# The third unit's q turned behind the second unit's first scores, where three idle products stood

## The chip, the cores and the metric

The kernel runs on one core of one Trainium2 chip. The metric is device time in microseconds (us) of one execution. A core has a matrix engine (PE, TensorE, with its weight loads shown apart as PEld), a vector engine (DVE), a scalar engine (ACT), GpSimd (POOL) and a queue (SP) that here does nothing but issue DMAs. Matrix products land in PSUM[...].

## The reference, cut to what matters

```python
batch, n_heads, seq, head_dim = (4, 8, 768, 48)
f = 1 / (1 + exp(-f_logit))
for t in range(S):                                   # gated outer-product recurrence
    state = f[:, :, t, :, None] * state + einsum('bhd,bhe->bhde', k[:, :, t], v[:, :, t])
    y[:, :, t] = einsum('bhd,bhde->bhe', q[:, :, t], state)
x = y.transpose(0, 2, 1, 3).reshape(3072, 384)       # tokens x (heads * head_dim)
h = x @ w_in                                         # 384 -> 2048
out = (h * (1 / (1 + exp(-1.702 * h)))) @ w_out      # 2048 -> 384
```

So there is a recurrence over the tokens of each head, and its output is the input of a two-layer block with a quick-gelu between. All is float32 in the kernel.

## The kernel before

**Units.** The tokens of a batch are cut into units of 256, three to a batch, twelve in all, numbered n = 0 to 11. Within a unit the recurrence is done without a loop over tokens: six levels (`level(l)`, l = 0 to 5) of doubling block length, each with 16 score products per unit (`score`, L384), a mask on the way out of PSUM (`evacuate`, L410, DVE), and 16 products of the masked scores with v (`add`, L448). After each level q and k, which lie in the tile `X`, are multiplied in place by running products of f (`promote`, L436 for k and L437 for q, DVE), and half of k is copied aside for the next level's scores (`set_aside`, tile `Kc`, L423, ACT). Then k is turned token-major (L505, L506), the chunk states are formed (L523, L540, L543), and the last part (L563) adds what earlier chunks contribute, copies y out of PSUM (L571, ACT) and sends it as `xT` to the layout that the two-layer block wants, by six DMAs on SP (L592, L597).

**Inputs.** Raw f, q and k of a unit are loaded token by token and must be turned to have the head's 48 channels on the partitions. For units 0, 1 and 2 (`N_FILL = 3`) this is done on PE: `turn` (L339) makes sixteen float32 products with the identity, in two PSUM tiles of eight, and ACT copies each tile out (L342). For the later units DVE transposes (L327). `begin_f`, `begin` and `begin_k` do f, q and k. `begin` does four things: the turn of q into `X[:, J]` (J alternates between 0 and 2 with n), two tiny POOL copies of the last token's q (L357, L358), and, for n > 0, the load of raw q of unit n+1 (`load_raw`, L258 or L251, four DMAs on SP). That load overwrites what the turn has read.

**Weights.** They come as 8-byte numbers. SP loads pieces into the tile `bits` (L180), ACT makes a first rescaled copy (`a`, L208), and DVE makes the float32 weight in five operations (L223 to L228). These run in the first quarter of the time, between the parts of the attention. The products of the two-layer block (`h`, L727, and `o`, L755; later `o_X` to `o_W`, L704) fill PE between the parts.

**Order.** PE's order is written out by hand throughout. Until the end of the fourth `merge` that is so for every engine: each executes its instructions in program order. From there on a planner orders the other engines. `parts_of(n)` makes the list of parts of unit n, into which the beginning of unit n+1 is inserted; `merge` goes through that list, and after each part puts so many columns of filling products and so many weight operations as its share says. For the second unit (n = 1) the list is: levels 0, 1, 2, 3, begin_f of unit 2, level 4, begin of unit 2, level 5, two turns of k to token-major, states, begin_k with the gates of unit 2. The first part of unit n also holds the last part of unit n-1 (`ahead`), ahead of its scores. `merge(1, ...)` has `hold=1`: no filling products are put behind its first part.

**Idle products.** `keep_up(times)` (L809) makes so many products of the identity with the masks, 384 columns wide, whose result nobody reads. There are two behind each of the first three levels of unit 0, and three behind level 0 of unit 1.

**SP around the place.** In program order after unit 0's six xT DMAs: v of unit 2 to a token-major scratch `v_tok` (L271), `vl` of unit 2 out of that scratch (L290), a weight piece (L180), another `vl`, and so on.

Of the kernel before, what the change touches and what calls it, by code (L numbers as in the profile page):

```python
# [23 lines left out]
def kernel(  # L24
# [34 lines left out]
    B, H, S, D = q.shape  # L59
# [216 lines left out]
    def load_vl(n, l):  # L276

        if n >= NALL:
            return
        t = vls[n, l] = ld.tile([P, DM], F32, tag=f"vl{l}", name=f"vl_{n}_{l}")  # L280
        if n < N_TURN:
            pt = ps.tile([P, DM], F32, tag="mm", name=f"tv_{n}_{l}", bufs=4)
            for g in range(NG):
                nc.tensor.matmul(
                    pt[g * 64:(g + 1) * 64], lhsT=perm[:, l - 1, :] if l else ident[:, ::2], rhs=vns[n][:, g, :],
                    start=True, stop=True,
                )
            nc.scalar.copy(t, pt)  # L288
            return
        nc.sync.dma_start(out=t, in_=v_toks[n % 2].rearrange("(n two m) e -> two n m e", two=2, m=LEV[l])[0])  # L290
# [513 lines left out]
    def keep_up(times):  # L804

        if times:
            pt = ps.tile([P, NL * 64], F32, tag="mm", name=f"idle_{next(serial)}", bufs=4)
        for _ in range(times):
            nc.tensor.matmul(pt, lhsT=ident, rhs=masks.rearrange("p l t -> p (l t)"), start=True, stop=True)  # L809
# [4 lines left out]
    def parts_of(n):  # L814

        parts = list(units[n][1])
        _, inter = parts.pop()
        if n:
            kind, scores = parts[0]
            _, ahead = units[n - 1][1][-1]  # L820
            parts[0] = kind, lambda: (ahead(), scores())
        if n < N_TURN:

            def with_v(l):
                kind, fn = parts[l]
                return kind, lambda: (fn(), load_vl(n, l) if n == 0 or l else None, keep_up(2 * (n == 0 and l < 3) or 3 * (n == 1 and l == 0)))
            parts[:NL] = [with_v(l) for l in range(NL)]
        if n + 1 < NALL:
            begin_f, begin, begin_k, begin_gates = units[n + 1][0]
            i = len(parts)  # L830
            if n + 1 < N_FILL:

                parts.append(("K", lambda: (begin_k(), begin_gates(), load_vl(n + 1, 0) if n + 1 < N_TURN else None)))
                parts.insert(i - 4, ("B", begin))
                parts.insert(i - 5, ("B", begin_f))
            else:
                kind, states = parts.pop()
                parts += [("B", begin_k), (kind, lambda: (states(), begin_gates()))]
                parts.insert(i - 3, ("B", lambda: (begin_f(), begin())))
        else:  # L840
            parts.append(("W", inter))
        return parts

    def merge(n, fill, columns, share, pieces=0, hold=0, by=1.0, chores=()):

        parts = parts_of(n)
        total = sum(share(kind) for kind, _ in parts)
        converting = {"W": 3, "T": 3, "B": 1} if n < N_FILL - 1 else {"W": 3, "V": 4, "S": 3, "T": 1, "B": 1}  # L850
# [88 lines left out]
```

## Time and profile before

| | |
|---|---|
| median of 6 runs | 657.23 us (656.44 to 661.18) |
| profiled execution, its own time | 657.87 us |
| its span, first to last instruction | 655.7 us |
| PE busy | 636.1 us (97%) |
| DVE, ACT, POOL busy | 444.6, 229.8, 55.0 us |
| mean granted TensorE clock | 0.997 of full |
| DMA traffic | 67.67 MB, mean 103 GB/s |

The profile is one execution. In it a row names line, engine, operation, output and inputs; an L number is a line of the kernel. A float32 product appears as two records, so a turn of sixteen products is 32 records and three idle products are six. Times in the timeline count from the span's start; neighbouring instructions of one line are merged in a row, with the number of records behind the x and, in brackets, how long the engine had stood idle before and what released it.

### The profile page before, as it was taken

How to read it: one execution, taken by the hardware profiler on the slowest of the kernel's cores; microseconds unless marked ns; L12 is line 12 of the kernel's file. 1: busy time of each engine (PE TensorE's matmuls, PEld its weight loads, DVE VectorE, ACT ScalarE, POOL GpSimd, SP SyncE). 2: the span in 40 equal slices, each digit the busy share in tenths (PEclk: the TensorE clock that was granted, in tenths of full speed). 3: DMA queues.
4: the chain of work that ended last, by engine and by line, in shares of the span. 5: the costliest groups of instructions: out<-in, count | busy, mean ns of one | idle time of the engine just before them, and what ended most of it. 6: DMA issues, size and time to landing. Idle time of an engine off the chain costs nothing.

```text
span 655.7 us, 20407 instructions
## 1 busy us (share of the span) xinstructions
PE 636.1 (97%) x8964; PEld 544.2 (83%) x8964; DVE 444.6 (68%) x802; ACT 229.8 (35%) x477; POOL 55.0 (8%) x116
## 2 busy tenths in 40 slices
PE   6988999999999999999999999999999999999997
PEld 5656767666678689989989989989989989989997
DVE  2988888788887657657658558558558557553571
ACT  3464443233223323324324324324324334222120
POOL 3020020020001002002002002002002002000000
PEclk9989999999999999999999999999999999999999
DMA  8886975284135545524514524605604202101000
GB/s 192 224 199 167 222 179 133 90 217 81 33 71 142 144 96 120 147 46 119 155 37 121 143 49 120 165 27 122 164 26 104 66 25 62 39 2 26 25 1 24
DMA packets 67554, 67.67 MB, mean 103 GB/s; under 512 B 30410, under 2 KB 61290, under 8 KB 67466
## 3 DMA queue, kind: packets, MB, share of 16 engines
q1 hardware_dynamic: 67466, 66.38, 40.4%
q8 instruction: 70, 1.15, 0.8%
q14 instruction: 18, 0.15, 0.1%
HBM read 56.92 MB, written 8.65 MB: 100 GB/s over the span
## 4 chain that ended last, share of the span: by engine, by line
PE 85%; DVE 9%; ACT 2%; issue 2%; DMA 1%; SPq 1%; DVEq 0%; ACTq 0%
PE h L727 36%; PE o L755 7%; PE o_X L704 7%; PE o_Y L704 7%; PE o_Z L704 7%; PE sc L384 5%; PE y L448 4%; PE o_W L704 4%; PE t L339 2%; PE y L563 2%; PE sc L523 1%; PE tkn L505 1%; DVE s L219 1%; DMA xT<-yT 1%; DVE X L439 1%
## 5 line engine op out<-in xcount | busy, mean ns | idle before, releaser
L727 PE MATMUL h<-xT,w_in 128*128 128x256 f32 (+1 forms) x1152 | 260.0, 381 | 5.2 <-DMA xT<-yT 2.5
L727 PEld LDWEIGHTS h<-xT,w_in 128*128 128x128 f32 x1152 | 215.2, 190 | 38.9 <-issue 4.4
L733 DVE TENSOR_TENSOR g<-h,sg 128x256 f32<-128x256 f32 (+1 forms) x192 | 80.9, 423 | 98.2 <-ACT sg L732 95.8
L732 ACT ACTIVATE sg<-h 128x256 f32<-128x256 f32 (+1 forms) x192 | 73.4, 384 | 192.5 <-PE h L727 185.6
L423 ACT COPY Kc<-X 128x512 f32<-128x512 f32 x69 | 46.1, 669 | 121.6 <-DVE X L439 84.0
L755 PE MATMUL o<-w_out,g 128*128 128x384 f32 x192 | 66.4, 493 | 0.0
L439 DVE TENSOR_TENSOR X<-X,tot 128x1024 f32<-128x1024 f32 x45 | 55.1, 1225 | 15.4 <-PE sc L384 10.2
L755 PEld LDWEIGHTS o<-w_out,g 128*128 128x128 f32 x192 | 35.2, 190 | 22.8 <-issue 1.5
L704 PE MATMUL o_X<-w_out,g 128*128 128x192 f32 x288 | 51.9, 329 | 0.0
L704 PE MATMUL o_Y<-T,S 128*128 128x192 f32 x288 | 51.1, 331 | 0.1
L704 PEld LDWEIGHTS o_Y<-T,S 128*128 128x128 f32 x288 | 46.5, 190 | 2.6 <-DVE u L679 1.2
L704 PEld LDWEIGHTS o_X<-w_out,g 128*128 128x128 f32 x288 | 47.3, 190 | 0.9
L410 DVE TENSOR_TENSOR A<-sc,masks 128x512 f32<-128x512 f32 x72 | 46.8, 680 | 0.0
L448 PE MATMUL y<-A,vl 64*48 64x64 f32 x2304 | 40.9, 217 | 0.1
L376 POOL TENSOR_TENSOR tot<-F 128x512 f32<-128x512 f32 x12 | 12.5, 1042 | 327.6 <-DVE st L540 327.6
L448 PEld LDWEIGHTS y<-A,vl 64*48 64x48 f32 x2304 | 36.1, 120 | 3.5 <-issue 3.1
L327 DVE STREAM_TRANSPOSE X<-raw 128x1024 f32<-128x1024 f32 x18 | 36.7, 2040 | 2.4 <-PE y L563 2.4
L571 ACT COPY yT<-y 48x512 f32<-48x512 f32 x48 | 27.8, 580 | 14.0 <-PE y L563 13.4
L384 PEld LDWEIGHTS sc<-X,Kc 48*64 48x64 f32 x1344 | 23.9, 134 | 8.5 <-ACT vl L288 4.0
L384 PE MATMUL sc<-X,Kc 48*64 48x64 f32 x1344 | 28.1, 219 | 1.7 <-DVE A L410 1.7
L376 POOL TENSOR_TENSOR tot<-tot 128x256 f32<-128x256 f32 (+4 forms) x60 | 27.6, 459 | 4.7
L704 PE MATMUL o_Z<-w_out,g 128*128 128x192 f32 x144 | 26.6, 331 | 0.0
(93 smaller groups left out, 663.8 us busy)
## 6 DMA issues: line engine op xcount, KB each, us to landing
vl<-v_tok SPq DMA_DIRECT2D x60, 192.0 KB, 2.7
bits<-in_moe_w_out_dram SPq DMA_DIRECT2D x8, 768.0 KB, 9.7
bits<-in_moe_w_in_dram SPq DMA_DIRECT2D x8, 576.0 KB, 7.4
v_tok<-in_v_dram SPq DMA_DIRECT2D x10, 384.0 KB, 4.3
vn<-v_tok SPq DMA_DIRECT2D x10, 384.0 KB, 6.8
xT<-yT SPq DMA_DIRECT2D x24, 144.0 KB, 2.8
raw<-in_f_logit_dram SPq DMA_DIRECT2D x18, 192.0 KB, 3.9
raw<-in_q_dram SPq DMA_DIRECT2D x18, 192.0 KB, 3.9
```

The costliest lines, as they stand in the source:

```text
L327: nc.vector.transpose(out.rearrange("p (a i j) -> p a j i", a=NP, j=R), raw[:, j].rearrange("p a (j d) -> p (a j) d", j=R)[:, :, :32],)
L376: nc.gpsimd.tensor_tensor(tn, t2[:, :, 0], t2[:, :, 1], ALU.mult)
L384: nc.tensor.matmul(out[g * HS:(g + 1) * HS, h, a, :], lhsT=lhs(h, a * U + g * G), rhs=rhs(h, a * U + g * G), start=True, stop=True,)
L410: nc.vector.tensor_tensor(A[:, :, c:c + w].rearrange("p h (x t) -> p h x t", t=64), t["sc"][:, :, c:c + w].rearrange("p h (x t) -> p h x t ...
L423: nc.scalar.copy(c.rearrange("p (n m) -> p n m", m=m), X[:, j, :NA].rearrange("p (n two m) -> p n two m", two=2, m=m)[:, :, hf, :],)
L439: nc.vector.tensor_tensor(qk, qk, by, ALU.mult)
L448: nc.tensor.matmul(dst(h, g, a), lhsT=vls[n, u][g * 64:(g + 1) * 64, (2 * a + h) * D:(2 * a + h + 1) * D], rhs=A(h, g, a), start=(start an ...
L704: nc.tensor.matmul(t[bank], lhsT=lhs(f), rhs=rhs(f), start=(new and f == 0), stop=(f == HF - 1), skip_group_check=True,)
L727: nc.tensor.matmul(ph, lhsT=w_in[:, c, ff * P:(ff + 1) * P], rhs=xTs[n][:, c, :], start=(c == 0), stop=(c == NK - 1))
L732: nc.scalar.activation(sg, ph, AF.Sigmoid, scale=1.702)
L733: nc.vector.tensor_tensor(g[ff // FG][:, ff % FG, :], ph, sg, ALU.mult)
L755: nc.tensor.matmul(t["po"], lhsT=g[ff // FG][:, ff % FG, tt * P:(tt + 1) * P], rhs=w_out[:, ff, :], start=(ff == ffs[0]), stop=(ff == ffs[ ...
```

## The change

For n = 1 the three idle products behind level 0 go, and `begin` of unit 2 (turn of q, the two POOL copies, the load of unit 3's raw q) is called there, at the end of the first part. At its old place, between level 4 and level 5, an empty part of the same kind stays, so that the shares which `merge` works out are unchanged. For n = 0 (the beginning of unit 1) everything is as before.

```diff
-                return kind, lambda: (fn(), load_vl(n, l) if n == 0 or l else None, keep_up(2 * (n == 0 and l < 3) or 3 * (n == 1 and l == 0)))
+                return kind, lambda: (fn(), load_vl(n, l) if n == 0 or l else None, keep_up(2 * (n == 0 and l < 3)))
...
             if n + 1 < N_FILL:
 
                 parts.append(("K", lambda: (begin_k(), begin_gates(), load_vl(n + 1, 0) if n + 1 < N_TURN else None)))
-                parts.insert(i - 4, ("B", begin))
+                parts.insert(i - 4, ("B", begin if n == 0 else lambda: None))
                 parts.insert(i - 5, ("B", begin_f))
+                if n:
+
+                    kind, head = parts[0]
+                    parts[0] = kind, lambda: (head(), begin())
```

## The prediction

> **What bounds the kernel now.** I read the slices of the page first, then the order of PE around the change, then the chain that ended last, then the clock and DMA traffic by stretch.
>
> The slices:
>
> ```profile
> PE   6988999999999999999999999999999999999997
> PEclk9989999999999999999999999999999999999999
> DMA  8886975284135545524514524605604202101000
> ```
>
> A slice is 655.7 / 40 = 16.4 us. PE has room only in the first four slices; by stretches it is busy 50.0 of 50 us almost everywhere from 200 us on. So PE work taken out of a full stretch shortens the end by its length, and PE work put into a hole costs nothing. DMA is heavy in slices 1 to 6 with a dip at the fourth (49 to 66 us).
>
> PE's timeline, at the new place (first six rows) and the old (last three):
>
> ```profile
> 45.08 1.13 PE L384 MATMUL sc<-X 48*64 48x64 f32 x32
> 46.14 3.00 PE L809 MATMUL idle<-masks,ident 128*128 128x384 f32 x6
> 49.08 0.70 PE L384 MATMUL sc<-X,Kc 48*64 48x64 f32 x32
> ...
> 51.80 0.67 PE L727 MATMUL h<-xT,w_in 128*128 128x256 f32 x2 [0.78 <-DMA xT<-yT]
> 53.21 2.40 PE L727 MATMUL h<-xT,w_in 128*128 128x256 f32 x10 [0.74 <-DMA xT<-yT]
> 55.54 0.70 PE L384 MATMUL sc<-X,Kc 48*64 48x64 f32 x32
> ...
> 69.96 1.97 PE L339 MATMUL t<-ident,raw 128*64 128x128 f32 x32
> 71.86 0.91 PE L755 MATMUL o<-w_out,g 128*128 128x384 f32 x2
> 72.70 0.70 PE L384 MATMUL sc<-X,Kc 48*64 48x64 f32 x32
> ```
>
> The idle products fill a gap before the second scores. Two waits for xT of unit 0, 0.78 and 0.74 us, follow. Nothing that PE does before 53.21 sets the time: the second half of xT does. At 69.96 the row has no bracket: the turn stands between products that were ready.
>
> The chain of waits says the same:
>
> ```profile
> 47.64 0.67 ACT Kc L423
> 48.31 0.94 ACT a L208 x2
> 49.24 0.29 SPq L592
> 49.58 3.50 DMA xT<-yT
> 53.21 1.12 PE h L727 x4
> ...
> 70.03 1.90 PE t L339 x32
> 71.93 0.84 PE o L755 x2
> ```
>
> The idle products are not on it, the turn of q is, with 1.90 us.
>
> **The change part by part.** *Turn of q out of its old place.* 32 records, 1.90 us in the chain (59 ns each). Does PE use this, or wait for another? The scores of level 5 move from 72.70 to 70.80. They need Kc, copied by ACT at 68.02 to 68.65, and the score bank, emptied by DVE at 68.45 to 69.06: both done. DVE is full from 59.8 to 72.2, then stands 1.25 us waiting for just these scores (before L437 at 73.46) and 0.98 us for a gelu input (at 77.88). In the new order the first wait vanishes and the second follows PE, so DVE comes along by 1.9 us in all. ACT loses two copies of 0.73 us. Until 95 us PE has no idle time of its own, so all 1.90 us should arrive. DVE as limit would leave about 1.25 us of it. I take 1.90.
>
> *Idle products out.* 6 records, 3.00 us, partly at half clock. Worth nothing by themselves: PE then waits 0.78 and 0.74 us for xT in any case, 1.52 us of cover for whatever takes their place.
>
> *Turn of q into the new place.* Its raw q was issued at 32.21 to 36.9, and such loads land after 2.7 us, so by 40; it waits for nothing. Its price depends on the clock, which is down here:
>
> ```profile
> 44.50:45.00 0.50, 0.50 (x26) 0.46 (x20) 0.40 (x2) 0.00 (x0) 0.37 (x1) 0.50 1.12 187
> 47.00:47.50 0.50, 0.50 (x2) 0.28 (x1) 0.50 (x2) 0.47 (x2) 0.42 (x2) 0.50 0.05 12
> 47.50:48.00 0.50, 0.50 (x2) 0.30 (x1) 0.50 (x2) 0.47 (x2) 0.49 (x1) 0.70 0.07 25
> 48.00:48.50 0.50, 0.50 (x3) 0.35 (x2) 0.50 (x2) 0.50 (x2) 0.35 (x2) 1.00 0.37 95
> ```
>
> (After the colon: length, busy time of PE, PEld, DVE, ACT, POOL, the granted clock, DMA share, GB/s.) The clock is 0.50 from about 44.4 and returns at about 47.8. The turn at half speed is in the trace too: at the start 53 records go from 4.42 to about 10.2, 109 ns each, then 42 more at 59 ns. From 46.14 to 47.8 that gives 15 records; the other 17 take 1.0 us: end at 48.8, where the idle products ended at 49.08.
>
> Here a rule speaks against the change. The Trainium skill, "TensorE: Matmul & The Clock Gate", Part 4, says the full clock does not engage for transposes in transpose mode, because these do not count as busy; Part 1 gives a free-running window of 3413 ns after which the clock is decided. This turn is an ordinary product against the identity, and the start of this trace has nothing but turns when the 109 ns become 59 ns. So the row says it counts. By the rule it would stay cold to 51.2 (47.8 + 3.4, an estimate from the page's window): 32 x 109 ns ends at 49.6, the scores double to 1.24 us (50.9), 0.45 us of y and 0.80 of v products, mostly warm, end at 52.3, the first two h records at 53.0. Still before 53.21: cost nothing. Cold for one window more (54.6): y 51.8, v products 53.4, two h records 54.4, the ten others 2.33 us to 56.8 instead of 55.54: cost 1.3 us. I take 0; ends 0 and 1.3.
>
> *ACT's two copies there.* They queue behind Kc of level 1 (47.64 to 48.31) and ahead of two weight copies (48.21, 1.02 us) and of Kc of level 2 (51.03). Copies at about 48.3 and 49.0, weight copies 49.7 to 50.7, then Kc at 51.03, which waits for DVE until then anyway. If they end 1 us later, Kc moves by 0.7 us; its reader on PE starts at 55.54, 3.8 us after Kc's end. The weight copies are first read by DVE at 55.11, 4.4 us of cover. Cost 0.
>
> *POOL's two copies,* 0.19 us each, go behind the gates of unit 1 (last ends 48.78) instead of at 72.81; POOL's next work is at 86.48. Cost 0.
>
> *Four DMAs of unit 3's raw q,* 2 x 192 + 2 x 176 = 736 KB, SP issue time 1.74 us. They leave 71.97 and enter SP behind v_tok (issued 50.84 to 51.45), ahead of the `vl` that stands at 55.17 because v_tok must land first: 3.6 us in which SP only waits. So no issue is delayed by SP itself. They pass `vl`, a weight piece (55.63), raw f and more. The traffic:
>
> ```profile
> 54.00:55.00 1.00, 1.00 (x6) 0.89 (x5) 0.23 (x1) 0.38 (x1) 0.00 (x0) 1.00 0.17 20
> 55.00:56.00 1.00, 1.00 (x31) 0.66 (x33) 1.00 (x4) 0.36 (x1) 0.00 (x0) 1.00 0.00 0
> 56.00:57.00 1.00, 1.00 (x53) 0.73 (x44) 1.00 (x4) 0.03 (x1) 0.00 (x0) 1.00 0.85 203
> ```
>
> 736 KB at the 227 GB/s seen at 53 us is 3.2 us, 2 us of it in this hole. xT's last DMA is issued by 50.8, ahead of it. The weight piece of 55.63: from 56 to 60 us 203 + 264 + 415 + 294 = 1176 KB moved, which is its 768 and two `vl` of 192, so it landed by 60; ACT reads it at 63.88. Some 1.5 us later is inside 3.9 us of cover. In exchange the queue, full from 63 to 90 us, loses 3.2 us of traffic, which may shorten PE's 0.99 us wait for the next xT at 95.08. Taken at 0; ends a loss of 0.5 us and a gain of 0.99 us.
>
> **Sum.** -1.90 + 0 + 0 + 0 = -1.90 us: span 655.7 to 653.8, own time of the profiled execution 657.87 to 655.97. That execution is 0.64 us above the median, so on the median 657.23 the forecast is **655.3 us**, 0.29% less.
>
> **The rivals.** *A, the clock stays down* for two windows: -1.90 + 1.3 = -0.6, 656.6 us. For it: the page's rule, and small products before it. Against: the start.
>
> *B, DVE takes the place of PE* between 72 and 95 us: only its 1.25 us of waiting is won, or nothing: 656.0 to 657.2 us. For it: DVE is busy without a break for 12 us. Against: both of its waits there are for PE.
>
> *C, the lighter DMA queue helps* too: up to 0.99 us more, 654.3 us; with part of the later waits of PE between 131 and 157 us (1.3 + 0.8 + 0.5 us, for ACT and DVE) under 653.9.
>
> *D, slower: the planner.* From the fifth merge on, the order of DVE, ACT and POOL comes from a planner that sees other times. A 2.04 us transpose (L327) put ahead of a 0.42 us gelu product (L733) on which PE waits costs up to 2.0 us a unit. Eight units at 0.5 us are +4, 659.3 us. It decides from 1.9 / 8 = 0.24 us a unit on. For it: DVE's order there is not fixed. Against: PE hides all of it now, with DVE at 68%.
>
> *E, the change does nothing:* the turn is on the chain with 1.90 us, so it would need its cost back at the new place; that place has 1.52 us of waits beyond the 3.0 us emptied.
>
> **How the numbers follow.** Forecast 56%, A 9%, B 9%, C 13%, D 13%. 0.5% is 3.3 us, about what a measurement of this kernel can tell from no change: below 653.9 faster, above 660.5 slower. C's far end with the spread of a median gives faster 0.12; D's worse half, with what I have not seen, slower 0.14; the rest, 0.74, is within. The forecast alone spans 654.6 to 656.0 us; the range takes in C's near part, A and B, and D's beginning: 653.9 to 658.0 us.
>
> **What would show it.** Right: 32 L339 records behind the scores at 46 us ending by 49, clock back at 47.8, h on the second xT half at 53.2 as before, level 5's scores at about 70.8, DVE's 1.25 us wait gone, everything from there 1.9 us earlier. Wrong: a clock of 0.5 past 48, h later than 53.2, an ACT wait for weights near 64, or PE below 50 of 50 us after 200 us.

## The result and the profile after

The changed kernel takes 656.21 us (median of 32 runs) beside 658.09 us for the kernel before (67 runs). The ratio over all runs, which is also that of their means, is 0.9965, 95% interval 0.9955 to 0.9975: 2.3 us less, between 1.6 and 3.0 (the medians lie 1.9 us apart). A second comparison on another chip (the run e11_changed below) gives 0.9959 (0.9944 to 0.9975). The forecast was 1.9 us less, 655.3 us.

The profiled execution of the changed kernel has a span of 654.1 us (own time 656.10), 1.6 us less than that of before. In the slices of its page PE's fourth (49 to 65 us) is fuller than before, 9 for 8, and the sixth (82 to 98 us) emptier, 8 for 9; the last 34 are as full as they were:

```profile
PE   6989989999999999999999999999999999999997
PEclk9989999999999999999999999999999999999999
DMA  8888875384034535614605605605604202101000
```

PE's timeline of the changed kernel, at the new place of the turn, at its old one, and at the next wait for xT (start, length, then the row; in brackets the idle time before and its releaser):

```profile
45.32 3.57 PE L339 MATMUL t<-ident,raw 128*64 128x128 f32 x32
48.82 0.70 PE L384 MATMUL sc<-X,Kc 48*64 48x64 f32 x32
...
51.31 0.67 PE L727 MATMUL h<-xT,w_in 128*128 128x256 f32 x2 [0.54 <-DMA xT<-yT]
52.82 2.40 PE L727 MATMUL h<-xT,w_in 128*128 128x256 f32 x10 [0.84 <-DMA xT<-yT]
...
67.44 2.85 PE L755 MATMUL o<-w_out,g 128*128 128x384 f32 x8
70.22 0.69 PE L384 MATMUL sc<-X,Kc 48*64 48x64 f32 x32
...
93.45 5.42 PE L727 MATMUL h<-xT,w_in 128*128 128x256 f32 x24 [1.79 <-DMA xT<-yT]
```

The turn takes 3.57 us here, not 1.90, and costs nothing: xT still ends the wait behind it. At the old place the `o` records run on without a break, and level 5's scores start at 70.22 instead of 72.70. But ahead of 93.45 PE waits 1.79 us for the second unit's xT, where it waited 0.99 (95.08 before); this is what the sixth slice shows.

**A table by stage.** The starts of the score rows (L384) in PE's timeline cut each execution into stages: A from the second unit's level 0 to its level 2 (the new place lies in it), B from level 2 to level 5 (the old place), C from level 5 to the third unit's level 0, D from there to the third unit's level 2 (the wait for the second unit's xT lies in it), and the rest to the end. All in us.

| run | start of A | A | B | C | D | rest |
|---|---|---|---|---|---|---|
| before | 45.08 | 10.46 | 17.16 | 14.24 | 13.49 | 555.27 |
| changed | 44.65 | 10.50 | 15.07 | 14.29 | 14.29 | 555.30 |
| e1_idle_out | 46.64 | 11.02 | 17.16 | 14.24 | 13.82 | 555.32 |
| e2_idle_behind | 44.97 | 13.16 | 14.76 | 14.30 | 14.96 | 555.35 |
| e3_load_stays | 44.06 | 10.07 | 15.23 | 14.31 | 16.61 | 555.42 |
| e4_twice | 45.65 | 10.72 | 17.17 | 14.30 | 14.50 | 555.26 |
| e5_full_stretch | 44.92 | 9.98 | 16.51 | 15.92 | 12.95 | 555.32 |
| e6_f_too | 44.69 | 9.90 | 13.75 | 15.65 | 13.30 | 555.31 |
| e7_k_behind_xT | 47.35 | 11.03 | 15.07 | 14.30 | 12.46 | 555.29 |
| e8_f_and_k | 44.63 | 11.46 | 13.74 | 15.25 | 12.46 | 555.56 |
| e9_k_alone | 45.18 | 11.98 | 17.19 | 14.23 | 12.47 | 555.25 |
| e10_q_stays_k_behind | 44.84 | 10.21 | 15.07 | 14.30 | 12.46 | 555.32 |
| e11_changed | 44.51 | 9.75 | 15.23 | 14.81 | 16.25 | 555.35 |
| e12_load_stays | 44.93 | 9.62 | 15.21 | 14.30 | 18.74 | 555.30 |

In the one pair of profiles: start -0.43 (ahead of the change, chance), A +0.04, B -2.09, C +0.05, D +0.80, rest +0.03; sum -1.60, the difference of the spans. B is the gain, and D gives part of it back. The start, A and D also differ between executions of one kernel (compare the two profiles of the changed one), so totals are judged by the ratios and stages by this table.

### The profile page after: what moved, and what is told of

Its sections match the earlier page's. It is cut to its first block, busy times and chain, and to the rows that moved or that the text cites. A ratio compares the mean times of both kernels' runs of the same rounds, so it can differ in the third digit from the quotient of the medians.

```text
span 654.1 us, 20397 instructions
## 1 busy us (share of the span) xinstructions
PE 634.6 (97%) x8958; PEld 543.1 (83%) x8958; DVE 444.7 (68%) x802; ACT 230.1 (35%) x477; POOL 60.3 (9%) x116
## 4 chain that ended last, share of the span: by engine, by line
PE 85%; DVE 8%; DMA 2%; SPq 2%; ACT 2%; issue 1%; DVEq 0%; ACTq 0%
PE h L727 37%; PE o_Y L704 8%; PE o_X L704 7%; PE o L755 7%; PE o_Z L704 7%; PE sc L384 5%; PE y L448 4%; PE o_W L704 4%; PE y L563 2%; PE sc L523 1%; PE tkn L505 1%; DMA xT<-yT 1%; DMA bits<-in_moe_w_in_dram 1%; DVE s L219 1%; SPq L251 1%
## 5 line engine op out<-in xcount | busy, mean ns | idle before, releaser
L704 PE MATMUL o_Y<-T,S 128*128 128x192 f32 x288 | 51.1, 331 | 0.1
L384 PEld LDWEIGHTS sc<-X,Kc 48*64 48x64 f32 x1344 | 23.8, 134 | 6.6 <-issue 4.2
L384 PE MATMUL sc<-X,Kc 48*64 48x64 f32 x1344 | 28.2, 220 | 0.2 <-DVE A L410 0.2
```

The lines of the kernel that those rows point to most:

```text
L384: nc.tensor.matmul(out[g * HS:(g + 1) * HS, h, a, :], lhsT=lhs(h, a * U + g * G), rhs=rhs(h, a * U + g * G), start=True, stop=True,)
L704: nc.tensor.matmul(t[bank], lhsT=lhs(f), rhs=rhs(f), start=(new and f == 0), stop=(f == HF - 1), skip_group_check=True,)
```

## The experiments

They came in three groups, each on one chip with its own runs of the kernel before (medians 658.52, 659.81 and 659.92 us), so ratios are compared rather than times.

### The idle products alone: e1_idle_out

```diff
-keep_up(2 * (n == 0 and l < 3) or 3 * (n == 1 and l == 0))
+keep_up(2 * (n == 0 and l < 3))
```

> Only the three idle products behind level 0 of the second unit go; the turn of q stays at its old place. Theory 'hole' (the gain is the turn's 1.90 us of PE time taken out of a full stretch): PE then waits about 3 us longer for xT and the time is that of before, ratio 1.000. Rival 'idle' (the gain comes from no longer running the idle products): ratio 0.9965, as in the changed kernel. Rival 'DMA' (the gain comes from the earlier load of raw q): 1.000. If the idle products are needed for the clock, it stays at 0.50 beyond 48.5 us and the first h products after 53 us run slow: up to 1.003.

Measured: 1.0025 (1.0011 to 1.0039), 1.6 us slower (0.7 to 2.6). Its PE timeline, and then two stretches of the clock (after the colon: length, busy time of PE, PEld, DVE, ACT, POOL, granted clock, DMA share, GB/s):

```profile
50.09 1.13 PE L384 MATMUL sc<-X,Kc 48*64 48x64 f32 x32 [2.69 <-ACT Kc L423]
51.01 1.07 PE L448 MATMUL y<-A,vl 64*48 64x64 f32 x32
52.01 1.55 PE L284 MATMUL tv<-vn,perm 128*64 128x384 f32 x4
53.56 4.17 PE L727 MATMUL h<-xT,w_in 128*128 128x256 f32 x12
```

```profile
48.00:49.00 1.00, 0.00 (x0) 0.00 (x0) 1.00 (x3) 0.96 (x3) 0.00 (x0) 1.00 0.03 5
50.00:51.00 1.00, 0.91 (x32) 0.91 (x36) 1.00 (x3) 0.95 (x3) 0.00 (x0) 0.50 0.74 163
55.00:56.00 1.00, 1.00 (x4) 0.82 (x3) 0.00 (x0) 0.00 (x0) 0.00 (x0) 0.50 1.28 208
```

PE stands still for 2.69 us, the clock halves from about 49.5 to 56.3, and the twelve h records that xT releases take 4.17 us instead of about 3. So the idle products were not worthless. The rival "idle" falls, and so does the forecast's zero for taking them out alone. That they help by keeping the clock up for what follows the wait is the reading of this one profile, and it does not account for all of the loss: stage A is 0.56 us longer in it than before. (In e9's profile, with the idle products in place, the clock fell there too, at 54.5.) In the change the turn of q fills the gap in their stead.

### Idle products kept behind the turn: e2_idle_behind

```diff
-parts[0] = kind, lambda: (head(), begin())
+parts[0] = kind, lambda: (head(), begin(), keep_up(3))
```

> The changed kernel with the three idle products kept, behind the turn of q. Theory 'hole': the second scores move from 48.8 to between 51.1 and 51.8, the two h records of the first xT half end at 53.6 to 54.3 rather than in time for 52.8, so the cover is overdrawn by 0.8 to 1.5 us: ratio 0.998 to 0.999. Rival 'idle': 1.000. Rival 'DMA': 0.9965.

Measured: 0.9964 (0.9950 to 0.9978), no worse than the change. A miss. The 51.1 to 51.8 us was worked out for half clock; in its profiled execution the clock was full there and the second scores start at 49.7, well ahead of xT. (A is long in that execution: xT's second half came 1.0 us later after the start of A than in the changed kernel's profile, and the clock fell at 54.4 us, behind two waits for xT of 0.93 and 0.91 us, so that the ten h records took 4.08 us instead of 2.40. The execution took 659.45 us beside the kernel's median of 656.97.) Whether the cover can be overdrawn was not settled.

### PE's products back at the old place: e4_twice

```diff
-parts.insert(i - 4, ("B", begin if n == 0 else lambda: None))
+parts.insert(i - 4, ("B", begin if n == 0 else again))
```

`again` makes the sixteen products of `turn` once more, of raw k, into PSUM, without copies.

> The changed kernel with sixteen more products at the old place, of the same shape as the turn of q (raw k against the identity), that nobody reads and nobody copies out. Theory 'hole': the 1.90 us come back, ratio 1.000. Rivals 'idle' and 'DMA': PE's 1.90 us there are covered, 0.9965 stays.

Measured: 1.0014 (0.9998 to 1.0030): the gain is gone. The row:

```profile
70.80 1.97 PE L811 MATMUL again<-ident,raw 128*64 128x128 f32 x32
72.70 0.91 PE L755 MATMUL o<-w_out,g 128*128 128x384 f32 x2
73.54 0.69 PE L384 MATMUL sc<-X,Kc 48*64 48x64 f32 x32
```

Stage B is back at 17.17. PE's time there is needed for the gain, and the early load of raw q, which this run keeps, wins nothing without it.

### Earlier, but into a full stretch: e5_full_stretch

```diff
 (the kernel before)
-parts.insert(i - 4, ("B", begin))
+parts.insert(i - 4, ("B", begin if n == 0 else lambda: None))
+if n:
+    kind, head = parts[2]
+    parts[2] = kind, lambda: (head(), begin())
```

> The kernel before, idle products and all, with the turn of q (its copies and its DMAs too) moved behind level 2 of the second unit, at about 57 us, where PE has filling products. Earlier, but not into a hole. Theory 'hole': ratio 0.9995 to 1.000 (there is one wait of 0.24 us near). Rival 'DMA': the load goes out into the thin stretch at 57 us, most of the gain is there, 0.998 or less. Rival 'idle': 1.000.

Measured: 1.0007 (0.9991 to 1.0022): nothing, as "hole" said; "DMA" would have had 0.998. But the zero is a sum. In the table A, B and D are shorter by 0.48, 0.65 and 0.54, and C is longer by 1.68, where PE waits for the second copy of k (`kn`), which stands on ACT behind a weight copy that waits 2.17 us for DVE:

```profile
80.90 0.68 PE L523 MATMUL sc<-vn,kn 64*64 64x48 f32 x32 [1.55 <-ACT kn L506]
```

So this run alone does not show that the early load is worth nothing; e4 does that.

### The load of raw q left where it was: e3_load_stays and e12_load_stays

The same kernel twice, on two chips.

```diff
 (begin)
-            if n:
+            if n and n != 2:
                 load_raw(n + 1, 1)
 (parts_of)
-parts.insert(i - 4, ("B", begin if n == 0 else lambda: None))
+parts.insert(i - 4, ("B", begin if n == 0 else lambda: load_raw(n + 2, 1)))
```

> The changed kernel, but the four DMAs of unit 3's raw q stay at their old place in SP's order, behind level 4. Theory 'hole': ratio 0.997, 1.9 us less than before, and the wait for the second unit's xT near 94 us is about 1.0 us as before, rather than 1.79. Rival 'DMA': the gain goes, 1.000. Rival 'idle': 0.9965.

> Once more the changed kernel with the four DMAs of raw q at their old place. Theory 'two limits': PE comes 1.9 us earlier to the wait for the second unit's xT, but xT doesn't, the wait there is over 2 us, and the ratio is 0.9985 to 1.000. Theory 'hole': the wait of 2.55 us and the slow clock behind it, seen in the first such run, were chance, and the ratio is 0.997.

Beside the second, the changed kernel itself was run (e11_changed):

> The changed kernel itself, beside the three runs below. Theory 'hole' (PE's 1.90 us alone) and theory 'two limits' (PE's products and the DMA queue up to the second unit's xT run out at nearly the same time near 93 us, so that both PE work and traffic must leave the stretch before it): both 0.9965.

Measured: 0.9998 (0.9984 to 1.0013) and 0.9991 (0.9968 to 1.0015); the changed kernel beside the second had 0.9959. PE's gain in B is there (15.23, 15.21), yet D grows to 16.61 and 18.74 and eats it: the wait is 2.55 and 3.49 us long instead of 0.99, and the 24 h records behind it take 6.99 and 8.16 us instead of 5.42. So the theory "hole" alone falls. PE's row at that wait in e12_load_stays, SP's timeline, and what SP waited for (total, times, longest):

```profile
94.70 8.16 PE L727 MATMUL h<-xT,w_in 128*128 128x256 f32 x24 [3.49 <-DMA xT<-yT]
```

```profile
85.97 0.59 SPq L592 DMA_DIRECT2D xT<-yT  x1
86.61 3.47 SPq L597 DMA_DIRECT2D xT<-yT  x2
91.71 0.52 SPq L592 DMA_DIRECT2D xT<-yT  x1
```

```profile
SPq L597 <- DMA vl<-v_tok: 2.4, 1, 2.4
SPq L592 <- DMA vn<-v_tok: 1.6, 1, 1.6
```

y is ready, but SP's xT issues stop twice until loads have landed that have no data in common with them. The program that kernel.py builds says why. SP's DMAs take eight semaphores in turn, and each issue waits until the DMA that had its semaphore before, the eighth before it, has landed (listed in SP's order; the two waits in the trace above are the third and the fourth xT line):

```
vl_5   <-v_tok    [waits DMAHW6]
vn     <-v_tok    [waits DMAHW7]
raw    <-in_k     [waits DMAHW0]   (four of these: 0, 1, 2, 3)
xT L592           [waits DMAHW4]
xT L597           [waits DMAHW5]
xT L597           [waits DMAHW6]   = vl_5 has landed
xT L592           [waits DMAHW7]   = vn has landed
xT L597           [waits DMAHW0]   = the first part of raw k has landed
xT L597           [waits DMAHW1]   = the second part
```

Raw k, issued just ahead, lands 10.7 us after issue here (9.0 in the changed kernel's first profile, 8.1 before). Two microseconds of PE don't help against that; less traffic ahead of it does. In e12_load_stays the clock also halves in the wait (0.50 from 93.4 to 100.3), hence the 8.16 us.

### The load of raw k behind xT: e9_k_alone, e7_k_behind_xT, e10_q_stays_k_behind

```diff
 (begin_k)
-            if n:
+            if n and n != 2:
                 load_raw(n + 1, 2)
 (parts_of)
-parts[0] = kind, lambda: (ahead(), scores())
+parts[0] = kind, lambda: (ahead(), load_raw(3, 2) if n == 2 else None, scores())
```

This edit on the kernel before is e9, on the changed kernel e7, on e12's kernel e10.

> The kernel before, with only the load of unit 3's raw k put behind the second unit's six xT DMAs. Theory 'two limits': the wait of 0.99 us for that xT goes, 0.9985, or 0.997 if the wait is longer in the mean than in the one profile. Theory 'hole', with xT's time taken as latency: 1.000.

> The changed kernel with the load of unit 3's raw k put behind the second unit's six xT DMAs on SP rather than ahead of them. If that xT lands late because the 736 KB of raw k stand before it in the DMA queues, the wait of 1.79 us near 93 us falls to under 0.5 us: ratio 0.9945. If the 3 to 4 us from issue to landing are latency, nothing moves: 0.9965.

> The turn of q moved, the load of raw q at its old place, the load of raw k behind xT. Theory 'two limits', with raw k as what xT queues behind: PE's 1.90 us and the wait of 0.99 us both come, 0.9955 or less, and it no longer matters where raw q is loaded. If raw q's traffic itself holds xT up, the wait stays over 1 us: 0.998. Theory 'hole': 0.997.

Measured: e9 0.9952 (0.9937 to 0.9968), e7 0.9932 (0.9906 to 0.9957), e10 0.9926 (0.9904 to 0.9947). D is 12.46 or 12.47 in all three. SP's timeline in e10, and PE's row:

```profile
86.97 1.21 SPq L597 DMA_DIRECT2D xT<-yT  x2
88.28 0.53 SPq L592 DMA_DIRECT2D xT<-yT  x1
88.86 1.22 SPq L597 DMA_DIRECT2D xT<-yT  x2
90.18 1.95 SPq L258 DMA_DIRECT2D raw<-in_k_dram  x4
```

```profile
91.50 5.45 PE L727 MATMUL h<-xT,w_in 128*128 128x256 f32 x24
```

SP issues xT without a stop (the eighth DMA before each is an older load now, and landed), and the h row has no bracket any more. With the way clear, it doesn't matter where raw q is loaded: e10 has it late and keeps all of PE's gain (0.9926 against e12's 0.9991). That confirms "two limits". Beside e9, on the same chip, e10 is another 1.8 us shorter (medians 656.33 and 654.55): with xT's way clear, PE's 1.90 us arrive nearly whole. e9 itself missed its forecast (0.9985, or 0.997): it gains 3.2 us by the ratio, where the one profile of before has a wait of 0.99 us. That this wait is often longer, with the slow clock behind it, would explain the rest, but it is not shown. In e1, which has the order of loads of before, the wait is 1.31 us at full clock, and D is only 1.4 us longer than e9's.

### The turn of f too: e6_f_too and e8_f_and_k

```diff
-parts.insert(i - 5, ("B", begin_f))
+parts.insert(i - 5, ("B", begin_f if n == 0 else lambda: None))
...
 parts[0] = kind, lambda: (head(), begin())
+kind1, head1 = parts[1]
+parts[1] = kind1, lambda: (head1(), begin_f())
```

e8 has the raw k edit as well.

> The changed kernel, and the turn of f of the third unit (with its load) moved too, from behind level 3 to behind level 1, where PE waits 0.54 and 0.84 us for xT in the changed kernel. Theory 'hole': 1.90 us leave a full stretch, of which 1.38 us lie in the waits, so some 1.4 us less than the changed kernel: ratio 0.9945. If the weight piece behind the load of raw f comes too late (it has 3 us of cover, the load is 3.2 us), ACT waits near 63.5 us and part is lost: 0.996. If the gain of the changed kernel was not a matter of PE's holes: 0.9965.

> Both moves of the two runs before together. If they are independent, their gains add: ratio 0.992 to 0.993 against the kernel before. If one uses the same hole as the other, less.

Measured: e6 0.9948 (0.9930 to 0.9965), e8 0.9919 (0.9892 to 0.9947). B falls by another 1.3 us, and C rises by 1.36 and 0.96. ACT's timeline in e6 shows why:

```profile
66.73 1.01 ACT L208 ACTIVATE a<-bits 128x384 f32<-128x384 f32 x2 [3.68 <-DMA bits<-in_moe_w_out_dram]
76.04 1.00 ACT L208 ACTIVATE a<-bits 128x384 f32<-128x384 f32 x2 [1.93 <-DMA bits<-in_moe_w_in_dram]
```

Weights now land too late for ACT, which holds up the copies of k behind them; PE then waits for `kn`:

```profile
77.56 0.68 PE L523 MATMUL sc<-vn,kn 64*64 64x48 f32 x32 [1.28 <-ACT kn L506]
```

Against the changed kernel's 0.9959 to 0.9965, e6 is not told apart. e8 has the lowest ratio of all, but its interval holds e7's and e10's: the raw k edit is the part shown to be worth having.

## Why the prediction was right, and where it was not

**The size is right, in part by luck.** -1.90 us was forecast, -2.3 (-1.6 to -3.0) measured. Two errors cancelled: PE's gain was taken to arrive by itself, and it does not; the move of the load was taken at nothing, and it is what lets the gain arrive. Rival E (nothing) and the slower outcome are out.

**Turn out of its old place: right.** 1.90 us forecast, B shows 2.09 and e4 gives them back. DVE came along: L437 follows L436 at once, and the second wait is 0.28 us instead of 0.98. Rival B falls.

```profile
71.15 0.68 DVE L436 TENSOR_TENSOR X<-X,tot 128x512 f32<-128x512 f32 x1
71.75 0.69 DVE L437 TENSOR_TENSOR X<-X,tot 128x512 f32<-128x512 f32 x1
...
75.45 0.42 DVE L733 TENSOR_TENSOR g<-h,sg 128x256 f32<-128x256 f32 x1 [0.28 <-ACT sg L732]
```

**"All 1.90 us should arrive" at 95 us: wrong.** The step argued that PE has no idle time until then. It left out that the next wait is for a DMA that does not come earlier because PE does. In e3 and e12, PE's two microseconds turn into a longer wait, with slow h records behind it. I had seen the 0.99 us wait and the full queue, and filed both under a possible gain.

**Four DMAs at zero: wrong.** Moving raw q is needed while raw k is queued ahead of xT: without it the ratio is 0.9991, with it 0.9959, on one chip (medians 659.55 and 656.88), some 2 us or more. It is not the whole of it: the chain of the changed kernel still goes through SP and xT.

```profile
87.05 0.58 SPq L597
87.64 0.04 issue
87.68 1.44 SPq L597
...
89.22 4.10 DMA xT<-yT
93.32 0.14 issue
93.45 5.42 PE h L727 x24
```

So rival C named the right wait, but the move of raw q did not take that wait away; it kept it from growing by all that PE had won.

**Idle products at zero: wrong alone, right in the change.** e1 loses 1.6 us; its 2.69 us gap cost the clock in the execution profiled, as far as one profile shows. The forecast looked at time on the path only.

**Turn at the new place: cost zero, right, by another course.** Forecast: half clock to 47.8, end at 48.8. In the profile the clock fell at 45.2 and came back near 48.6, past the 48 us that the prediction had named as a sign of being wrong:

```profile
45.00:45.50 0.50, 0.50 (x27) 0.41 (x19) 0.00 (x0) 0.49 (x2) 0.42 (x2) 0.73 0.39 71
47.00:47.50 0.50, 0.50 (x8) 0.50 (x6) 0.50 (x2) 0.50 (x2) 0.43 (x1) 0.50 0.05 18
48.50:49.00 0.50, 0.50 (x15) 0.28 (x15) 0.50 (x2) 0.00 (x0) 0.00 (x0) 0.85 0.29 72
```

Thus the whole turn ran cold, 3.57 us, ended at 48.8 all the same because it began 0.8 us earlier, and the clock rose with little but the turn running. So the rule of the Trainium skill ("TensorE: Matmul & The Clock Gate", Part 4) that transposes do not count as busy does not reach these ordinary products. (At the start of the kernel, from which the prediction took the same, the granted clock in the rows reads 1.00 while a record takes 109 ns; there only the length of the records tells.)

**Rival A: its condition came, its cost did not.** In the profiled executions of e4 and e7, which have the same turn at the same place, the clock stayed down twice as long, from 44.7 to 51.6 and from 46.0 to 52.8. The wait for xT covered that too. In e4:

```profile
46.76 3.68 PE L339 MATMUL t<-ident,raw 128*64 128x128 f32 x32
...
54.04 2.40 PE L727 MATMUL h<-xT,w_in 128*128 128x256 f32 x10 [0.58 <-DMA xT<-yT]
```

In e7 PE waits 0.93 us at this place. What is out is rival A's loss of 1.3 us.

**ACT, POOL, the first weight piece: right.** Kc of level 2 starts at 50.51, ACT reads the piece at 63.49 without waiting. A later piece has become tight (0.33 us of wait at 76.33, 1.03 in e11); in e11, C is 0.6 us longer than before (14.81 beside 14.24).

**Rival D: out.** The rest is 555.25 to 555.56 us in all fourteen profiles; what the planner orders did not move.

## What to carry to other kernels

Work moved from a full stretch into a gap is won only up to the next wait that is not for the engine relieved: look up what that wait ends on, and whether it can come earlier too. If it is a DMA, ask what is issued just ahead of it on its queue and which earlier DMAs its issue waits for; a load that nobody needs for a while belongs behind it, and that one move was worth as much here as the change itself (e9 0.9952, e11 0.9959, not told apart). Before filler work is called free to remove, ask what the clock does in the gap that it leaves.

## What the runs showed that I had not expected

- An urgent DMA of small size was held at issue by the landing of the slow load eight places ahead: 0.5 us in the changed kernel's first profile, 2.4 and 1.6 us in e12, nothing with raw k behind.
- PE gaps shorter than the window of 3413 ns that the Trainium skill gives ("TensorE: Matmul & The Clock Gate", Part 1) were followed by half clock: 2.12 us (e11), 2.69 us (e1), even two of 0.93 and 0.91 us close together (e2). Others were not: 1.79 us (the changed kernel's first profile), 2.01 us (e4), 2.47 us (e2, later). So the length of the gap does not decide. A fall can cost nearly as much as the wait, as in e11's row, beside e2's at full clock:

```profile
93.52 7.11 PE L727 MATMUL h<-xT,w_in 128*128 128x256 f32 x24 [2.12 <-DMA xT<-yT]
...
96.80 5.42 PE L727 MATMUL h<-xT,w_in 128*128 128x256 f32 x24 [2.47 <-DMA xT<-yT]
```

- What the traces show instead is a grid in time. From the granted clock of short stretches one can work out when the clock changed: the row 45.00:45.50 above has 0.73, so 0.23 us of it were at full clock and 0.27 at half, and the clock fell at 45.23. It fell and rose at 44.38 and 47.80 us before, at 45.23 and 48.65 in the changed kernel, at 49.45 and 56.28 in e1, at 54.45 and 57.86 in e2. In each of the twelve profiles with such changes (e6 and e8 have none) they lie whole multiples of 3.41 us apart, the length of that window. Cut on this grid, between 9 and 106 us, every full-clock window in which PE was busy for 0.55 of the time or less was followed by half clock, and none above 0.65; in between both occurred. A half-clock window was followed by full clock when PE was busy for 0.93 or more, and by another at half clock at 0.91 or less. The 2.12 us of e11 lie in one window, busy for 0.38; the 2.47 us of e2 lie across a boundary and leave windows of 0.69 and 0.59. These shares are an estimate from the profile's PE times, whose ends are modelled, and no run was made to vary them. The grid lies differently in each execution, so whether a gap of this size costs the clock is partly chance.
